# Four weight loads moved to another queue, and a later block's input made ahead of other steps

## The chip, the cores and the metric

The kernel runs on one core of a Trainium2 chip. Its engines are TensorE (PE in the profile, with its weight loads shown apart as PEld), VectorE (DVE), ScalarE (ACT), GpSimd (POOL) and SyncE (SP, which here only issues DMAs). The metric is the device time of one execution in microseconds (us); lower is better. Before the change the median of three runs is 349.3 us (348.23, 349.3, 350.38).

## The reference

A chunked linear attention (a decayed state scan) feeds a gated feed-forward layer.

```python
# x (4, 8, 768, 32), a (4, 8, 768), B and C (4, 8, 768, 16)
for c in range(768 // 32):
    cum = np.cumsum(la, axis=-1)                      # la = log of the clipped a
    L = np.exp(cum[..., :, None] - cum[..., None, :]) * causal
    M = np.einsum('bhin,bhjn->bhij', Cc, Bc) * L
    y_intra = np.einsum('bhij,bhjd->bhid', M, xc)
    y_inter = np.einsum('bhin,bhnd->bhid', Cc, state) * np.exp(cum)[..., None]
    y[:, :, sl] = y_intra + y_inter
    state = decay_full * state + sum_j(B_j x_j * decay_from_j)
# x = y as (3072, 256); w_gate, w_val (256, 1536); w_out (1536, 256)
g = x @ w_gate
out = (g * sigmoid(g) * (x @ w_val)) @ w_out
```

## The kernel before, in words

The 768 steps of the sequence are cut into six blocks of 128 (k = 0 to 5), each with all four batches, so a block's x for the feed-forward layer is 256 features by 512 tokens. The layer's 1536 hidden features are twelve groups of 128 (f = 0 to 11).

**Steps and their names.** Every piece of work is added to a planner (class `Plan`, lines 45 to 191) with a name, which is used below and in the lists of the code. For a block k of the attention: "L k b" is the decay scan of batch b on DVE, "S k" the scores on PE, "M k p" the mixing of scores and decays on DVE (`mix`, line 419), "y k" the values and carried part on PE (lines 519 to 549), "ap k q" a new state's copy out of PSUM, "step k q" the state recurrence on DVE (`step`, line 476, four instructions). The x that the layer reads is split into a high part "xh" and a low part "xl" (lines 574 and 586), each in four pieces i for k > 0. For the layer: "gv k f m" is the gate (m = 0) or value (m = 1) matmul group on PE (line 666), "si k f" the silu on ACT (line 677), "pr k f" the product on DVE (line 682); "hh" and "hl" are the high and low part of the hidden values, "po" the output matmuls. PSUM has four banks for gv and po, so gv 1 2 0 needs the bank that si 1 0 lets go.

**Weights.** There are 18 weight pieces of 512 KB: twelve for the gate and value weights (wg0 to wg11, i = 0 to 11) and six for the output weights (wo0 to wo5, i = 12 to 17). Each is 64-bit data from which the kernel makes a rounded high part and a low part. Its steps are "raw i" (the load, `w_fetch`, line 599), "mag i" and "rest i" (ACT, lines 606 and 620), "range i" (mostly POOL, line 616), "shift i", "sign i", "round i" (DVE, lines 627 to 637), "wh i" (ACT, line 639), for i < 9 "minus i" (ACT) and a POOL accumulating DMA "wl i", for the others "wl i" on DVE (line 647). The raw pieces share eight buffers (`RAW`), so a ninth load waits until the first piece's round has read its buffer; the working tile w of the output weights has one buffer, so mag 13 comes after wl 12. Block 0 uses the first nine groups in full fp32 from the piece's own tile, with x whole ("xf 0" to "xf 5", on ACT), and only from group 9 on the split form.

**Who sets the order.** SP issues the loads of raw 0 to 11 and the attention's inputs ("bc", "xb", "aj", and "E", the decays for the state, which has one buffer). Two DMAs that write the clipped decays back to DRAM, named "written" and "written e", and raw 12 to 17 are issued by ACT. The planner simulates all engines, takes the ready step of lowest rank at each point, and so writes one program order for each engine. `plan.follow(order)` makes each step of a list wait in the plan for the one before it to be issued; `plan.fix(e, names)` does so for an engine's own list. Lists for DVE, Act, Pool and PE stand in `FRONT` (lines 1000 to 1028) and hold until about 62 us of the run; after them, and on SP, ranks decide. Each engine then runs its instructions in that order. All engine calls go through the helper `Ordered`, whose line 202 is therefore the line of nearly every instruction in the profile.

Of the kernel before, what the change touches and what calls it, by code (L numbers as in the profile page):

```python
# [28 lines left out]
NF = DFF // P  # L29
# [15 lines left out]
class Plan:  # L45
# [19 lines left out]
    def add(self, engine, cost, run, rank, needs=(), takes=(), uses=(), gives=None, kind=None, lag=0.0, rows=1.0, slack=0.0):  # L65
        engines = [(engine, cost)] if cost is not None else engine
        self.ops.append(Op(engines, run, rank, needs, takes, uses, gives, kind, lag, rows, slack, cost is None))
# [145 lines left out]
def scan_moe_kernel(ctx: ExitStack, tc, aj, an, bc, xb, wgv, wo, cst, own, first_e, out):  # L213
    nc = tc.nc
    PSUM = bass.MemoryType.PSUM
    te, ve, se, ge, sp = (
        Ordered(tc, e) for e in (nc.tensor, nc.vector, nc.scalar, nc.gpsimd, nc.sync)
    )

    def pool(name, bufs, stack=ctx, **kw):  # L220
        return stack.enter_context(tc.tile_pool(name=name, bufs=bufs, **kw))
# [5 lines left out]
    raw = pool("raw", RAW)  # L227
# [323 lines left out]
    xh, xl = {}, {}  # L551
# [44 lines left out]
    NW = len(pieces)  # L596
# [50 lines left out]
    def w_low(i):  # L647
        _, his, los, j, name = pieces[i]
        hi = part[i]["hi"]
        if i < WHOLE:  # L650
            lo = part[i]["lo"]
# [14 lines left out]
    def gate_val(k, f, m):  # L666
        t = hid.setdefault((k, f), {})["gv"[m]] = ps_mm.tile([P, T], F32, tag="mm", name=f"gv{k}_{f}_{m}")
        if not k and f < WHOLE:
            w = part[f]["w"].bitcast(F32).rearrange("p (a b c) -> p a b c", b=2, c=P)
# [55 lines left out]
    rest = {}  # L725
# [29 lines left out]
    def do(f, *a):  # L755
        return lambda *e: f(*a, *e)


    plan = Plan(
        dict(mm=4, at=4, L=1, E=1, bc=1, xb=1, Cz=1, T=2, raw=RAW, w=1, xh=2, xl=2, sg=SG, ob=2),  # L760
        dict(SP=3.3, Act=3.0, DVE=1.0, PE=1.5, Pool=2.0, Page=0.0, **{"-": 0.7}),
    )
    add = plan.add
# [10 lines left out]
    def due(k, f=0):  # L774

        return begin[k] + f * (GV if k else PACE0)

    def at(n):

        return divmod(n, NF)  # L780

    def due_sum(k, f):
        return begin_sum[k] + f * PO
# [5 lines left out]
    for n, ranks in enumerate(IDLE):  # L789
        for i, r in enumerate(ranks):  # L790
            need = [("idle", n, i - 1)] if i else IDLE_AFTER[n]
            takes = [] if i else [("at", ("rest", n))]
# [2 lines left out]

    for i in range(NW):
        r = due(0, i) - 1.0 if i < NF else due_sum(0, 2 * (i - NF)) - 1.0
        if i < NF:
            add("SP", 0.48, do(w_fetch, i), r - 9.0, takes=[("raw", ("raw", i))], gives=("raw", i), lag=SHARED.get(i, 1.3))
        else:  # L800
            add("Act", 0.1, do(w_fetch, i, se), due(*at(LAST[i - NF])) + 2, [("si", *at(LAST[i - NF]))], takes=[("raw", ("raw", i))], gives=("raw", i), lag=1.3)
        add("Act", 0.57, do(w_magnitude, i, "Act"), r - 5.5, [("raw", i)], takes=[("sg" if i < NF else "w", ("w", i))], gives=("mag", i))
        far = i in FAR
        e, c = ("Pool", 2.2) if far else ("DVE", 0.335)
        add(e, c, do(w_range, i, ge if far else ve), r - 4.5, [("mag", i), *([("round", i - 1)] if i == 1 else [])], gives=("range", i))
        add("Act", 0.57, do(w_rest, i, "Act"), r - 4.5, [("raw", i), *([("xf", 5)] if i == 3 else [])], gives=("rest", i))
        add("DVE", 0.335, do(w_shift, i), r - 4.2, [("range", i)], gives=("shift", i))
        gate = ()
        if not i:
            n, gate = slice(0, 2 * P), [("round", 0, "gate")]  # L810
            add("DVE", 0.35, do(w_sign, i, n), r - 3.9, [("shift", i)], gives=("sign", 0, "gate"))
            add("DVE", 0.35, do(w_round, i, n), r - 3.3, [("sign", 0, "gate"), ("rest", i)], uses=[("raw", i)], gives=gate[0])
        n, c = (slice(2 * P, 4 * P), 0.35) if not i else (slice(0, 4 * P), 0.6)
        add("DVE", c, do(w_sign, i, n), r - 3.9, [("shift", i), *gate], gives=("sign", i))
        add("DVE", c, do(w_round, i, n), r - 3.3, [("sign", i), ("rest", i)], uses=[("raw", i)], gives=("round", i))
        if i < WHOLE:
            r = due(1, i) - LATER
        add("Act", 0.57, do(w_high, i, "Act"), r - 2.7, [("round", i), ("gv", 0, 0, 0)], gives=("wh", i))
        whole_done = [("gv", 0, i, m) for m in range(2)]
        if i < WHOLE:  # L820
            add("Act", 0.57, do(w_minus, i), r - 2.6, [("round", i), ("gv", *at(MINUS[i]), 0) if MINUS[i] else ("ap", 1, 1)], gives=("minus", i))
            add("Pool", 1.2, do(w_low, i), r - 2.5, [("wh", i), ("minus", i), *whole_done], uses=[("w", i)], gives=("wl", i), lag=1.6)
        else:
            add("DVE", 0.6, do(w_low, i), r - 1.5, [("wh", i)], uses=[("w", i)], gives=("wl", i))
# [10 lines left out]
    for k in range(NB):  # L835
        r = due(k)
        SLACK = min(k / 2, 1.0)
        z = -5 if not k else r + LEAD[min(k, 3)]
        L, E, BC, XB, CZ, TT = ("L", k), ("E", k), ("bc", k), ("xb", k), ("Cz", k), ("T", k)
# [14 lines left out]
        if not k:  # L854
# [4 lines left out]
            for b in range(BATCH):  # L859
                r = z + 0.5 + b  # L860
# [56 lines left out]
        if not k:  # L917
            add("-", 0.0, new_whole, -9, [("clip", 1)], takes=[("xl", "xf")], gives="xf")
            add("-", 0.0, do(new_x, 0), due(0, WHOLE) - 9, [("xf", i) for i in range(6)], takes=[("xh", ("xh", 0)), ("xl", ("xl", 0))], gives=("x", 0))
            for g in range(2):  # L920
                r = due(0, WHOLE) - 7 + 2 * g
                add("Act", 0.57, do(first_high, g, "Act"), r, [("x", 0)], gives=("xh", 0, g))
# [11 lines left out]
    for k in range(NB):  # L934
        xs = [(t, k, i) for t in ("xh", "xl") for i in range(2 * K if k else 2) if k or t == "xh" or not i]
        for f in range(NF):
            r = due(k, f)
# [14 lines left out]
            r = due_sum(k, f) - 4  # L952
# [4 lines left out]
        for n, (m, t, fs) in enumerate(sums_of(k)):  # L957
# [4 lines left out]
            r = due_sum(k, fs[0]) + n * 0.01  # L962
            c = 0.7 * len(fs) * (t[1] - t[0]) / T
            add("PE", c, do(project, k, m, t, fs), r, need, takes=[] if fs[0] else [("mm", b)], uses=[b, *(("h", k, f) for f in fs)], gives=prev, kind="r")
            if fs[-1] == NF - 1:
# [1 line left out]
                c = 0.6 * (t[1] - t[0]) / T  # L967
                add([("Act", c), ("DVE", c)], None, do(drain, k, m, t), r + 0.5, [prev], takes=[("ob", o)], uses=[b, o], gives=o)
                add("SP", 0.48, do(store, k, m, t), r + 2, [o], uses=[o], gives=("stored", k, m, t), lag=0.9)
    plan.follow([("raw", i) for i in range(NW)])  # L970
    for steps in ORDER:
        plan.follow(steps)
    for e, names in FRONT.items():
# [11 lines left out]
FETCH = dict(aj=10.0, an=35.0, bc=12.0, xb=31.0)  # L985
LATER = 3.0
WHOLE = 9
LAST = (5, 6, 9, 10, 11, 12)
MINUS = (3, 3, 4, 5, 5, 5, 10, 10, 10)
FEW = 8  # L990
# [13 lines left out]
sign 2, round 2, shift 3, sign 3, round 3, pr 0 1, shift 4, sign 4, round 4, step 0 1, shift 5, pr 0 2, sign 5, round 5,  # L1004
shift 6, sign 6, round 6, pr 0 3, shift 7, sign 7, round 7, shift 8, sign 8, pr 0 4, round 8, L 1 0, L 1 1, L 1 2, pr 0 5,
L 1 3, shift 9, bt 1, sign 9, M 1 0, pr 0 6, round 9, M 1 1, M 1 2, ce 1, M 1 3, pr 0 7, wl 9, shift 10, sign 10, round 10,
shift 11, pr 0 8, ap 1 0, wl 10, step 1 0, sign 11, round 11, pr 0 9, step 1 1, wl 11, shift 12, sign 12, round 12, pr 0 10,
xh 1 0, xh 1 2, xl 1 0, xl 1 1, xl 1 2, xl 1 3, wl 12, pr 0 11
""",
    Act="""  # L1010
by batch, Cz 0, mag 0, E 0, ap 0 0, rest 0, written, mag 1, xf 0, xf 1, xf 2, xf 3, xf 4, xf 5, rest 1, mag 2, rest 2, si 0 0,
mag 3, rest 3, mag 4, rest 4, mag 5, si 0 1, rest 5, mag 6, ap 0 1, written e, rest 6, mag 7, rest 7, si 0 2, mag 8, Cz 1, rest 8,
xh 0 0, si 0 3, xh 0 1, wh 0, minus 0, wh 1, minus 1, si 0 4, mag 9, rest 9, wh 2, minus 2, wh 3, si 0 5, raw 12, wh 4,
mag 10, rest 10, wh 5, wh 6, wh 7, wh 8, si 0 6, raw 13, minus x 0, minus x 1, mag 11, si 0 7, rest 11, minus 3, minus 4, wh 9,
si 0 8, mag 12, rest 12, rest 13, minus 5, wh 10, ap 1 1, si 0 9, raw 14, wh 11, si 0 10, raw 15, minus 6, minus 7, minus 8,
wh 12, xh 1 1, xh 1 3, rest 14, si 0 11, raw 16, mag 13, si 1 0, raw 17, hh 0 0, rest 15
""",
    Pool="""
clipped, range 0, range 3, range 4, range 5, range 6, range 7, range 8, wl 0, range 9, wl 1, wl 2, range 10, xl 0 0, range 11,
# [11 lines left out]
SHARED = {9: 6.1, "aj": 2.4, 10: 1.9}  # L1031
# [58 lines left out]
```

## Time and profile before

| | |
|---|---|
| median of three runs | 349.3 us (348.23 to 350.38) |
| profiled execution | 347.7 us, of which the span of the trace is 345.6 us |
| PE busy | 340.6 us (99%) |
| DVE busy | 225.9 us (65%) |
| ACT busy | 124.2 us (36%) |
| POOL busy | 45.5 us (13%) |
| chain that ended last | PE 86%, DVE 9%, issue 3%, DMA 1% |
| granted TensorE clock | full (1.0) over the span |

All times inside the profile are in us from the start of the span. A timeline row gives the start, the time taken, the engine, the operation, the tiles written and read (out<-in), and how many instructions were merged into the row. ACTq and SPq rows are the issues of DMAs, not the transfers. The instructions of one engine overlap a little: a 0.68 us DVE instruction is followed by the next one 0.60 us after its start.

### The profile page before, as it was taken

The numbers are of one execution on the slowest core, as the hardware profiler recorded it, in microseconds if no ns is written. First come the engines' busy times: TensorE is split into PE (matmuls) and PEld (weight loads), VectorE is DVE, ScalarE is ACT, GpSimd is POOL, SyncE is SP. The second block draws the span as 40 slices with busy tenths as digits, with TensorE's granted clock in tenths as the row PEclk, the third lists the DMA queues.
The fourth block names the chain that finished last, engine by engine and source line by source line (L and its number), as shares of the span: only waits on it lengthen the run. The fifth ranks groups of instructions, "written<-read, shape, count | busy, mean of one in ns | idle before, by whom it ended". The sixth has DMA issues, their size and how long they took to land.

```text
span 345.6 us, 7433 instructions
## 1 busy us (share of the span) xinstructions
PE 340.6 (99%) x3207; PEld 267.1 (77%) x3207; DVE 225.9 (65%) x399; ACT 124.2 (36%) x231; POOL 45.5 (13%) x36
## 2 busy tenths in 40 slices
PE   8999999999999999999999999999999999999996
PEld 7644457788788888887888878888888888888895
DVE  7999999979599763675582686454676440565320
ACT  4699766742445502212312212322222221222221
POOL 2389763220321000000000000000000000000000
PEclk9999999999999999999999999999999999999999
DMA  7899976980002811000651000392000000100001
GB/s 247 298 378 284 247 147 195 236 234 0 1 4 87 212 71 62 0 2 2 186 124 61 0 2 2 108 185 78 2 0 3 4 0 3 58 2 0 0 2 61
DMA packets 9983, 30.98 MB, mean 90 GB/s; under 512 B 1311, under 2 KB 2111, under 8 KB 9311
## 3 DMA queue, kind: packets, MB, share of 16 engines
q1 hardware_dynamic: 7192, 24.23, 23.2%
q0 software_dynamic: 1440, 2.88, 4.6%
q10 hardware_dynamic: 1319, 3.41, 3.1%
q8 instruction: 25, 0.41, 0.5%
q14 instruction: 7, 0.06, 0.1%
HBM read 24.28 MB, written 3.35 MB: 80 GB/s over the span
## 4 chain that ended last, share of the span: by engine, by line
PE 86%; DVE 9%; issue 3%; DMA 1%; ACT 0%; DVEq 0%; ACTq 0%
PE gv L202 49%; PE po L202 29%; PE y L202 4%; PE S L202 2%; DVE L L202 2%; DVE sg L202 2%; PE a L202 1%; DVE T L202 1%; DMA rows<-in_aj 1%; DVE wg4w L202 1%; DVE wg3w L202 0%; DVE wg5w L202 0%; DVE wg6w L202 0%; DVE wg9w L202 0%; DVE wg10w L202 0%
## 5 line engine op out<-in xcount | busy, mean ns | idle before, releaser
L202 DVE TENSOR_TENSOR sg<-gv,sg 128x512 f32<-128x512 f32 x72 | 49.6, 689 | 77.4 <-PE gv L202 76.6
L202 ACT ACTIVATE sg<-gv 128x512 f32<-128x512 f32 x72 | 43.1, 598 | 109.8 <-PE gv L202 109.8
L202 DVE TENSOR_TENSOR hh<-sg,hh 128x512 fp32r<-128x512 f32 x72 | 49.9, 696 | 13.5 <-ACT hh L202 12.3
L202 ACT CAST hh<-sg 128x512 fp32r<-128x512 f32 x31 | 19.3, 622 | 27.1 <-PE po L202 20.6
L202 DVE TENSOR_TENSOR_SCAN L<-L,dj 128x520 f32<-128x520 f32 x20 | 23.9, 1242 | 2.5 <-DMA L<-clipped 2.5
L202 ACT COPY ob<-po 128x512 f32<-128x512 f32 (+1 forms) x13 | 7.2, 555 | 48.6 <-PE po L202 48.1
L202 DVE CAST hh<-sg 128x512 fp32r<-128x512 f32 x41 | 17.4, 427 | 2.3 <-PE po L202 1.2
L202 DVE TENSOR_TENSOR L<-S,L 128x512 f32<-128x512 f32 x24 | 15.1, 682 | 0.3 <-PE S L202 0.3
L202 PE MATMUL po<-hh,wo4h 128*128 128x512 f32 (+1 forms) x52 | 15.2, 376 | 0.0
L202 PE MATMUL po<-hh,wo2h 128*128 128x512 f32 (+1 forms) x52 | 15.2, 375 | 0.0
L202 PE MATMUL po<-hh,wo0h 128*128 128x512 f32 (+1 forms) x52 | 15.2, 375 | 0.0
L202 PE MATMUL po<-hh,wo5h 128*128 128x512 f32 (+1 forms) x52 | 15.1, 373 | 0.0
L202 PE MATMUL po<-hh,wo3h 128*128 128x512 f32 (+1 forms) x52 | 15.0, 373 | 0.0
L202 PE MATMUL po<-hh,wo1h 128*128 128x512 f32 (+1 forms) x52 | 15.0, 373 | 0.0
L202 PE MATMUL y<-L,xb 64*32 64x64 f32 x768 | 11.3, 236 | 0.1
L202 PEld LDWEIGHTS y<-L,xb 64*32 64x32 f32 x768 | 9.2, 112 | 2.9 <-issue 2.1
L202 PEld LDWEIGHTS po<-hh,wo0h 128*128 128x128 f32 x52 | 9.5, 188 | 1.9 <-issue 0.2
L202 PEld LDWEIGHTS po<-hh,wo3h 128*128 128x128 f32 x52 | 9.5, 188 | 1.7
L202 PEld LDWEIGHTS po<-hh,wo5h 128*128 128x128 f32 x52 | 9.5, 188 | 1.7
L202 PEld LDWEIGHTS po<-hh,wo1h 128*128 128x128 f32 x52 | 9.5, 188 | 1.7
L202 PEld LDWEIGHTS po<-hh,wo2h 128*128 128x128 f32 x52 | 9.4, 188 | 1.8
L202 PEld LDWEIGHTS po<-hh,wo4h 128*128 128x128 f32 x52 | 9.4, 188 | 1.7
(302 smaller groups left out, 749.3 us busy)
## 6 DMA issues: line engine op xcount, KB each, us to landing
L<-clipped SPq DMA_DIRECT2D x10, 520.0 KB
xb<-in_xb SPq DMA_DIRECT2D x6, 768.0 KB, 11.1
bc<-in_bc SPq DMA_DIRECT2D x6, 512.0 KB, 3.3
out<-ob SPq DMA_DIRECT2D x11, 256.0 KB, 5.4
E<-clipped SPq DMA_DIRECT2D x5, 260.0 KB
wg0r<-in_wgv SPq DMA_DIRECT2D x1, 512.0 KB
wg1r<-in_wgv SPq DMA_DIRECT2D x1, 512.0 KB
wg2r<-in_wgv SPq DMA_DIRECT2D x1, 512.0 KB
```

Of the source, the lines that this page charges most:

```text
L202: ins = getattr(self.engine, name)(*a, **k)
```

## The change

The loads raw 4 to 7 go from SP's queue to ACT's, and leave SP's list; they stand in ACT's order at four places. In DVE's order the x of block 1 (the second block) comes ahead of step 1 1 and of shift, sign and round of piece 12; in ACT's order xh 1 1 and xh 1 3 come ahead of minus 8, and wh 12 behind raw 16.

```diff
     for i in range(NW):
         r = due(0, i) - 1.0 if i < NF else due_sum(0, 2 * (i - NF)) - 1.0
-        if i < NF:
+        if i in BESIDE:
+            add("Act", 0.1, do(w_fetch, i, se), r - 9.0, takes=[("raw", ("raw", i))], gives=("raw", i), lag=SHARED.get(i, 1.3))
+        elif i < NF:
             add("SP", 0.48, do(w_fetch, i), r - 9.0, takes=[("raw", ("raw", i))], gives=("raw", i), lag=SHARED.get(i, 1.3))
...
-    plan.follow([("raw", i) for i in range(NW)])
+    plan.follow([("raw", i) for i in range(NW) if i not in BESIDE])
+    plan.follow([("raw", i) for i in BESIDE])
...
+BESIDE = range(4, 8)
...
     DVE="""
...
-shift 11, pr 0 8, ap 1 0, wl 10, step 1 0, sign 11, round 11, pr 0 9, step 1 1, wl 11, shift 12, sign 12, round 12, pr 0 10,
-xh 1 0, xh 1 2, xl 1 0, xl 1 1, xl 1 2, xl 1 3, wl 12, pr 0 11
+shift 11, pr 0 8, ap 1 0, wl 10, step 1 0, sign 11, round 11, pr 0 9, wl 11, pr 0 10, xh 1 0, xh 1 2, xl 1 0, xl 1 2, xl 1 1, xl 1 3,
+step 1 1, shift 12, pr 0 11, sign 12, round 12, wl 12
 """,
     Act="""
-by batch, Cz 0, mag 0, E 0, ap 0 0, rest 0, written, mag 1, xf 0, xf 1, xf 2, xf 3, xf 4, xf 5, rest 1, mag 2, rest 2, si 0 0,
+by batch, Cz 0, mag 0, E 0, ap 0 0, rest 0, written, raw 4, mag 1, raw 5, xf 0, xf 1, xf 2, raw 6, xf 3, xf 4, xf 5, raw 7, rest 1, mag 2, rest 2, si 0 0,
...
-si 0 8, mag 12, rest 12, rest 13, minus 5, wh 10, ap 1 1, si 0 9, raw 14, wh 11, si 0 10, raw 15, minus 6, minus 7, minus 8,
-wh 12, xh 1 1, xh 1 3, rest 14, si 0 11, raw 16, mag 13, si 1 0, raw 17, hh 0 0, rest 15
+si 0 8, mag 12, rest 12, rest 13, minus 5, wh 10, ap 1 1, si 0 9, raw 14, wh 11, si 0 10, raw 15, minus 6, minus 7,
+xh 1 1, xh 1 3, minus 8, rest 14, si 0 11, raw 16, wh 12, mag 13, si 1 0, raw 17, hh 0 0, rest 15
```

## Rows read from the trace of the kernel before

**Rows 1.** Busy time by stretch: stretch, length, then each engine (x instructions).
```profile
36.65:48.29 11.64, 11.64 (x90) 5.45 (x89) 11.64 (x15) 9.09 (x18) 7.48 (x7) 1.00 0.96 220
48.29:60.90 12.61, 12.04 (x294) 9.54 (x293) 12.44 (x29) 7.05 (x16) 5.19 (x5) 1.00 0.65 167
```

**Rows 2.** Chain that ended last, in order of time: start, length, what.
```profile
60.90 33.04 PE gv L202 x144
```

**Rows 3.** Timeline at y 1: the last mix step, and PE's weight loads.
```profile
47.98 0.68 DVE L202 TENSOR_TENSOR L<-S,L 128x512 f32<-128x512 f32 x1
...
48.78 0.55 PEld L202 LDWEIGHTS y<-L,xb 64*32 64x32 f32 x45 [0.25 <-issue]
```

**Rows 4.** Timeline 55 to 62 us: the steps around block 1's x.
```profile
55.75 0.62 ACT L202 CAST wg11h<-wg11w 128x512 fp32r<-128x512 f32 x1 [2.35 <-DVE wg11w L202]
...
56.23 0.86 DVE L202 SCALAR_TENSOR_TENSOR T<-T,E 128x64 f32<-128x64 f32 x4
56.27 0.59 ACT L202 ACTIVATE sg<-gv 128x512 f32<-128x512 f32 x1
56.62 0.86 PE L202 MATMUL y<-L,xb 64*32 64x64 f32 x64
...
59.41 0.68 DVE L202 TENSOR_TENSOR sg<-gv,sg 128x512 f32<-128x512 f32 x1
...
59.83 0.61 PE L202 MATMUL gv<-xh,wg11l 128*128 128x512 f32 x2
60.01 0.74 DVE L202 CAST xh<-y 128x256 fp32r<-128x256 f32 x2
...
60.90 0.70 PE L202 MATMUL gv<-xh,wg0h 128*128 128x512 f32 x2 [0.45 <-DVE xh L202]
...
61.99 0.68 DVE L202 TENSOR_TENSOR wo0l<-wo0w,wo0h 128x512 fp32r<-128x512 f32 x1
```

**Rows 5.** Timeline: E's load, the next output piece and silu, weigh_c of block 2.
```profile
58.76 0.63 SPq L202 DMA_DIRECT2D E<-clipped  x1
...
62.77 0.67 ACT L202 ACTIVATE wo1w<-wo1r 128x512 f32<-128x512 f32 x1 [1.03 <-DVE wo0l L202]
...
63.35 0.58 ACT L202 ACTIVATE sg<-gv 128x512 f32<-128x512 f32 x1
...
84.66 0.69 DVE L202 TENSOR_TENSOR bc<-bc,E 128x512 f32<-128x512 f32 x1
```

**Rows 6.** Timeline of ACT at the start: "written", rest 0, the second xf group.
```profile
12.29 0.33 ACTq L202 DMA_DIRECT2D clipped<-all  x1
...
12.71 0.67 ACT L202 ACTIVATE wg0r<-wg0r 128x512 int32<-128x512 uint32 x1
...
14.85 0.76 ACT L202 COPY xf<-y 128x256 f32<-128x256 f32 x3 [0.33 <-PE y L202]
```

**Rows 7.** Transfers in 10 to 12.3, 12.3 to 16, 16 to 20, 20 to 24.
```profile
DMA packets 109, 0.37 MB, mean 159 GB/s; under 512 B 13, under 2 KB 21, under 8 KB 109
...
q1 hardware_dynamic: 317, 1.16, 97.7%
...
DMA packets 553, 1.63 MB, mean 407 GB/s; under 512 B 61, under 2 KB 181, under 8 KB 552
...
q10 hardware_dynamic: 135, 0.09, 7.5%
...
DMA packets 452, 1.67 MB, mean 417 GB/s; under 512 B 52, under 2 KB 52, under 8 KB 447
```

**Rows 8.** Timeline of SP's issues: raw 10.
```profile
22.34 0.33 SPq L202 DMA_DIRECT2D wg10r<-in_wgv  x1
```

**Rows 9.** Timeline 24 to 27 us: mag 7, si 0 2, pr 0 2.
```profile
23.95 0.67 ACT L202 ACTIVATE wg7w<-wg7r 128x512 f32<-128x512 f32 x1
...
25.07 0.60 ACT L202 ACTIVATE sg<-gv 128x512 f32<-128x512 f32 x1
...
26.99 0.68 DVE L202 TENSOR_TENSOR sg<-gv,sg 128x512 f32<-128x512 f32 x1
```

## The prediction

> **What bounds the kernel now.** I read the busy times by stage first. TensorE (PE) is busy in all 11.64 us between 36.65 and 48.29, and VectorE (DVE) too; between 48.29 and 60.90 PE is busy 12.04 of 12.61 us, DVE 12.44 [rows 1]. So PE sets the time, and DVE is close behind it until 60.9 us. Then I read the chain that ended last: back from the end it is PE alone as far as 60.90, where one piece of 33.04 us with 144 matmuls starts, 0.459 us for two [rows 2]. Ahead of 60.90 it runs through DVE. A gain must come from an idle moment of PE before that point, and a loss needs DVE, ScalarE (ACT) or a transfer to be late for PE.
>
> Two such moments are to be seen. At y 1, the values of the second block (k = 1), PE's weight loads pause 0.25 us before 48.78, just when DVE finishes the last mix step M 1 3 (47.98 + 0.68 = 48.66) [rows 3]. Here DVE has nothing to spare: what DVE loses earlier, PE loses here. The other is at 60.90: gv 1 0 0 waits 0.45 us for xh, which DVE made at 60.01; the second block's x was complete on PE at 56.62 + 0.86 = 57.48 already [rows 4]. This is the stall that the new DVE order can reach.
>
> **Second block's x made earlier.** The steps ahead of xh in DVE's list are now step 1 1, wl 11, shift 12, sign 12, round 12, pr 0 10. From 56.23 (step 1 1) to 59.41 (pr 0 10) is 3.18 us; one step of the 0.68 us form takes 0.60 from start to start (59.41 to 60.01), so without wl 11 the four moved steps hold 2.58 us [rows 4]. After the change only wl 11 and pr 0 10 stand there. wl 11 waits for wh 11, which ACT ends at 55.75 + 0.62 = 56.37: say 56.42. pr 0 10 follows at 57.02; its silu ends at 56.27 + 0.59 = 56.86. xh starts at 57.62, after y's end at 57.48; its two casts take 0.74, and casts and four xl together 1.98 (60.01 to 61.99, where wl 12 follows) [rows 4], so xh is complete at 58.36 and xl at about 59.6. ACT's two xh now precede minus 8 and can start near 57.9 as well. PE wants xh one pair after 59.83, at 60.29, and xl two pairs later, at 61.21. Both are ready 1.5 us or more before that. PE starts at 60.29 and not at 60.90: **0.61 us gained**, the most this part can give. Its lower bound is 0.
>
> **What the moved steps make late.** DVE starts step 1 1 at 59.60; with pr 0 11 now among them, the four moved steps take 2.58 + 0.60 to the next start, 62.78, and round 12 ends some 0.08 behind that, the overlap of the 0.68 us form: 62.86. step 1 1 is the last user of the single E buffer. E's load for the third block, issued by SP at 58.76, must wait for it until about 60.5, 1.7 us, and at worst xb's load behind it on SP as well. The first reader, ce 2 on DVE, is at 84.66 [rows 5]: 22 us of cover; at 0 in the sum. The state itself is read no earlier than the third block's carried part.
> Behind round 12 ACT is in order: wh 12 (0.62, as wh 11), then mag 13, which shares one buffer with wl 12 (0.68, DVE), then si 1 0. mag 13 started at 62.77, 0.10 after wl 12 ended (61.99 + 0.68 [rows 4]), and si 1 0 0.58 later, at 63.35 [rows 5]. That makes 62.86 + 0.05 + 0.62 + 0.05 + 0.68 + 0.10 + 0.58 = 64.94 for si 1 0, ended at 65.52 (0.58 long), against 63.93 now. It frees the bank that gv 1 2 0 needs, twelve pairs after 60.29, or 65.80. The cover is thus only 0.28 us, and each 0.1 us by which DVE or ACT run later than this costs PE 0.1. Bounds: 0 and 0.6; I take 0.1, since the sum of the spacings comes out just in time.
>
> **Four loads issued by ACT.** ACT gets four DMA issues of about 0.33 us: raw 4 and 5 around mag 1, raw 6 between xf 2 and xf 3, raw 7 after xf 5. If each held the engine up, the three before xf 3 would cost 1.0 us less the 0.33 that ACT idles there for PE [rows 6], and raw 7 another 0.33: up to 1.0 us. I take 0: the issue "written" of the same list stands behind rest 0, and yet it was issued at 12.29 while rest 0 began at 12.71 [rows 6]; ACT's sequencer is ahead of its engine, and each of the new issues has queued work in front of it. SP loses four issues, so raw 8 can go out right behind raw 3 while fresh buffers are left, and raw 7 then takes the buffer of raw 0, whose last reader is round 0; nothing that raw 7 waits for stands behind it on ACT. The start of gv 0 0 0 is set by xf, not by SP; nothing is gained there.
>
> **When the four pieces land.** raw 4 to 7 now come after raw 8. A piece is 0.524 MB. From 12.3 us the transfers moved 1.16, 1.63 and 1.67 MB up to 16, 20 and 24 us, after 0.37 MB between 10 and 12.3 [rows 7]. Served in order of issue (raw 2, 3, 8, written, 4, 5, 6, 7), raw 7 is complete with 7 x 0.524 + 0.09 = 3.76 MB, at 20 + 4 x (3.76 - 3.16) / 1.67 = 21.4. The old raw 7, sixth, is complete by the same count at 20.2; raw 10, for which the queue's waits name it as the last releaser, was issued at 22.34 [rows 8], so landing took 2.1 us more at most. So the new one lands by 23.5, and mag 7 is at 23.95 [rows 9]. By the same count raw 4 and 5 may keep ACT waiting some 1 us; si 0 2, the first of its steps that DVE would miss, has 1.3 us of cover (below). Cost 0.
> Order of issue is what the row says: "written", issued on ACT's queue at 12.29 [rows 6], moved nothing up to 16 us: all 317 packets of that window are of SP's q1, and the 135 of ACT's q10 came in the next [rows 7]. The Trainium skill, "DMA: Bandwidth & Descriptors", section "Queues, rings and completion order", says that each DMA engine takes turns between the queues it has work for, a packet each. This trace does not bear it out from the moment of issue; once q10's packets did flow, both queues moved at once, as it says. What turns would do here is the first rival.
>
> **Sum.** -0.61 + 0.1 + 0 = -0.5 us. The profiled execution took 347.7 us (span 345.6), 1.6 below the median of 349.3; a shift of the span applies to both: 347.2 there and 348.8 as the median. A measurement of this kernel can tell about 1%, 3.5 us, from no change.
>
> **Rivals.**
> *Late pieces, slower.* If ACT's queue and SP's shared one to one from raw 3 on, raw 7 would be complete when 0.524 + 2 x 2.19 = 4.9 MB have moved, just after 24 us (4.83 by then [rows 7]), and land with 2.1 more at 26.3: mag 7 2.35 us late. si 0 2 follows 1.12 behind and would end at 25.67 + 2.35 = 28.0; pr 0 2 stands in order on DVE at 26.99 [rows 9], 1.3 us of cover. DVE loses 1.05, has no slack up to M 1 3, and PE loses it at y 1: +1.05 - 0.5 = +0.5, 349.8. If the pieces also started as late as "written" did, after 16, and took 3 us each, mag 7 would come near 28.7, the loss would be 3.4 and the time 352.2. It decides from a landing at 25.3; slower than before from 25.9. For it: these are the pieces that were moved behind another. Against it: rows 7. Chance 0.12, with some 0.03 of it above 1%.
> *No gain, PE waits elsewhere.* The stall at 60.90 goes, but si 1 0 behind mag 13 is late by more than 0.28, and gv 1 2 0 gives the 0.6 back: 349.3. For it: the thin cover above; against it: the spacings, which come out in time by it. Chance 0.15.
> *Issues not hidden.* ACT holds xf up by some 0.7: -0.5 + 0.7 = +0.2, 349.5. Against it: rows 6. Chance 0.06.
> *More gained.* DVE, less hindered by GpSimd at other instants, also removes the 0.25 us at y 1 [rows 3]: -0.75 and, with a luckier order later, -1.2: 348.1. Chance 0.10.
> My forecast, a gain of 0.3 to 0.6: 0.57.
>
> **Numbers.** 348.8 us. Each case but the worst end of the first rival lies between 348.1 and 349.8; the three runs before spread 1.1 to either side of their median, so I take 346.9 to 350.6. Faster by over 1%: 0.02, since PE idles only 0.57 us in the stage [rows 1] and its work is untouched. Slower by over 1%: 0.04. Within: 0.94.
>
> **What would show it.** gv 1 0 0 directly behind gv 0 11 1, with no wait for xh, near 60.3; xh on DVE near 57.6; step 1 1 after xl, E's load near 60.5; ACT's four issues between 12.6 and 15.6 with xf and gv 0 0 0 still at 14.85 and 15.1; raw 8 on SP near 11.2; no wait of ACT for wg7r; PE's piece after 60.3 unbroken. Wrong would be: ACT waiting for wg6r or wg7r and DVE for si 0 2; a pause of PE at gv 1 2 0; or M 1 3 ending well after 48.7.

## The result and the profile after

The changed kernel took 354.03 us (median of 4 runs, 353.62 to 354.5) against 349.43 us for the kernel before on the same chip (4 runs, 348.23 to 350.38): a ratio of 1.0132, with an interval of 1.0098 to 1.0166. The forecast of 348.8 us and its range up to 350.6 were wrong; the change costs 4.6 us. Medians and ratios leave out single executions in a slower state of the chip; four of the kernels below have one such execution each. The profiled execution of after took 353.74 us with a span of 351.6 us, 6.0 more than the profiled span before; the pair differs by more than the medians because the profiled execution before, 347.7 us, is one of that kernel's faster ones.

The first view is the chain that ended last (start, length, what). Where it had been DVE and PE ahead of 60.90 [rows 2], it is now one transfer: raw 7, from its issue by ACT at 16.06 to ACT's first reading of it at 32.24.

```profile
16.06 16.16 DMA wg7r<-in_wgv
32.22 0.02 issue
32.24 0.66 ACT wg7w L202
32.90 0.55 ACT wg7r L202
33.45 0.49 ACT sg L202
...
33.98 9.90 PE gv L202 x16
...
64.32 35.59 PE gv L202 x156
```

The list of waits (who waited for whom: us in total, times, longest) shows three engines stopped by it, one behind the other. Before, ACT had no wait for any of the four pieces; after, it waits for raw 4 and raw 5 too (0.59 and 0.80 us).

```profile
DVE sg L202 <- ACT sg L202: 5.9, 1, 5.9
...
ACT wg7w L202 <- DMA wg7r<-in_wgv: 4.8, 1, 4.8
...
PE gv L202 <- ACT sg L202: 3.4, 1, 3.4
...
ACT wg6w L202 <- DMA wg6r<-in_wgv: 1.4, 1, 1.4
```

The timeline gives the places. The first three rows are mag 7, si 0 2 and pr 0 2, which answer to [rows 9]: 8.29, 8.28 and 6.97 us later than there. The fourth is gv 0 4, both groups. The last three are block 1's x on DVE, the last pair of gv 0 11 1 and the first of gv 1 0 0, which answer to [rows 4].

```profile
32.24 0.66 ACT L202 ACTIVATE wg7w<-wg7r 128x512 f32<-128x512 f32 x1 [4.83 <-DMA wg7r<-in_wgv]
...
33.35 0.58 ACT L202 ACTIVATE sg<-gv 128x512 f32<-128x512 f32 x1
...
33.96 0.69 DVE L202 TENSOR_TENSOR sg<-gv,sg 128x512 f32<-128x512 f32 x1 [5.87 <-ACT sg L202]
...
33.98 6.47 PE L202 MATMUL gv<-xf,wg4w 128*128 128x512 f32 x8 [3.40 <-ACT sg L202]
...
64.22 0.76 DVE L202 CAST xh<-y 128x256 fp32r<-128x256 f32 x2 [0.74 <-PE y L202]
...
66.65 0.62 PE L202 MATMUL gv<-xh,wg11l 128*128 128x512 f32 x2
...
67.10 0.62 PE L202 MATMUL gv<-xh,wg0h 128*128 128x512 f32 x2
```

PE lost time twice here. It waited 3.40 us for a bank that si 0 2 had to free, and then gv 0 4 took 6.47 us where the same eight matmuls take 3.60 elsewhere. The busy times by stretch (columns as in [rows 1]; the number after POOL is the granted clock) show why: after the pause, in which PE was busy 0.02 of 2 us, the clock was granted at 0.50, the lower level of 1.2 GHz, in all of 34 to 38 us and, by the means of 0.69 and 0.60, in parts of the stretches beside it.

```profile
32.00:34.00 2.00, 0.02 (x1) 0.02 (x1) 0.04 (x1) 1.76 (x4) 1.02 (x1) 0.69 0.99 252
34.00:38.00 4.00, 4.00 (x5) 1.84 (x6) 3.90 (x7) 4.00 (x8) 3.07 (x2) 0.50 0.73 281
38.00:40.00 2.00, 2.00 (x4) 0.82 (x3) 1.93 (x5) 2.00 (x5) 0.84 (x1) 0.60 0.28 97
```

How late PE is against before, at one piece after another, is the ledger of the change:

| PE starts | before | after | later by |
|---|---|---|---|
| gv 0 0 0 | 15.08 | 15.80 | 0.72 |
| gv 0 3 0 | 26.26 | 26.99 | 0.73 |
| gv 0 4 0 | 29.69 | 33.98 | 4.29 |
| gv 0 5 0 | 33.13 | 40.28 | 7.15 |
| y 1 1 | 55.78 | 62.61 | 6.83 |
| gv 1 0 0 | 60.90 | 67.10 | 6.20 |

So 3.56 are the wait (3.40 by the list), 2.86 the lower clock; 0.32 come back up to y 1 1, most of it at y 1, where M 1 3 is now done before PE gets there, and 0.63 at gv 1 0 0.

The transfers of 16 to 20, 20 to 24 and 24 to 28 us show how raw 7 came late (packets, MB, share of the 16 DMA engines' time; q1 is SP's queue, q10 ACT's).

```profile
q10 hardware_dynamic: 433, 1.21, 79.0%
q1 hardware_dynamic: 99, 0.34, 20.9%
...
q1 hardware_dynamic: 223, 0.85, 52.4%
q10 hardware_dynamic: 223, 0.81, 50.0%
...
q1 hardware_dynamic: 129, 0.73, 92.0%
q10 hardware_dynamic: 48, 0.15, 14.2%
```

Up to 20 us the older DMAs go first: SP's "bc" for block 1, issued at 15.97, hardly moves while ACT's raw 4 to 6, issued at 13.05 to 14.30, are served; most of q1's 99 packets there are raw 8's. From 20 to 24 both queues flow and take turns, 223 packets each. By 24 us q10 had moved 2.02 of the 2.19 MB it had been given ("written" and four pieces). Then SP's next transfer, L of block 1, gets in. In 24 to 28 the 129 packets of q1 took 92% of 64 engine-us, 0.46 us each, against 0.15 each in the stretch before; the trace has L's packets at 8,320 bytes and 0.5 to 0.9 us, the pieces' at 4,096 bytes and 0.16 us. The last 0.17 MB of ACT's pieces needed until 32 us.

### The profile page after: what moved, and what is told of

Its sections match the earlier page's. It is cut to its first block, busy times and chain, and to the rows that moved or that the text cites. A ratio compares the mean times of both kernels' runs of the same rounds, so it can differ in the third digit from the quotient of the medians.

```text
span 351.6 us, 7435 instructions
## 1 busy us (share of the span) xinstructions
PE 343.4 (98%) x3207; PEld 268.6 (76%) x3207; DVE 223.4 (64%) x396; ACT 126.3 (36%) x234; POOL 44.9 (13%) x36
## 4 chain that ended last, share of the span: by engine, by line
PE 89%; DMA 5%; ACT 1%; issue 0%; ACTq 0%
PE gv L202 55%; PE po L202 28%; DMA wg7r<-in_wgv 5%; PE y L202 4%; PE S L202 2%; ACT wg7w L202 0%; ACT wg7r L202 0%; ACT sg L202 0%; ACT ob L202 0%; ACTq L202 0%
## 5 line engine op out<-in xcount | busy, mean ns | idle before, releaser
L202 DVE TENSOR_TENSOR hh<-sg,hh 128x512 fp32r<-128x512 f32 x72 | 49.7, 696 | 13.9 <-ACT hh L202 12.7
L202 ACT CAST hh<-sg 128x512 fp32r<-128x512 f32 x33 | 20.5, 622 | 22.3 <-PE po L202 14.7
```

What stands on the lines that cost most here:

```text
L202: ins = getattr(self.engine, name)(*a, **k)
```

## The experiments

**The two halves apart.** First the order half alone: all loads on SP as before.

```diff
-BESIDE = range(4, 8)
+BESIDE = range(0)
-... written, raw 4, mag 1, raw 5, xf 0, xf 1, xf 2, raw 6, xf 3, xf 4, xf 5, raw 7, rest 1, ...
+... written, mag 1, xf 0, xf 1, xf 2, xf 3, xf 4, xf 5, rest 1, ...
```

> Only the second half of the change: the new order of DVE and ACT around the second block's x; raw 4 to 7 are issued by SP as before. If the four moved loads are the whole loss, PE has no wait at gv 0 4 0, gv 1 0 0 follows gv 0 11 1 without a pause, and the time is 0.4 to 0.7 us below the kernel before (near 348.9, ratio 0.998). If the new order has a part in the loss, it is slower than before by 0.5 us or more.

Measured: 349.47 us, ratio 1.0009 (0.998 to 1.0038). The expected gain, 0.2% of the time, is smaller than this interval can show. The profiled span is 345.2, 0.4 less than before, and gv 1 0 0 follows gv 0 11 1 with no wait. But in ACT's part of the timeline a new wait stands, of which more below:

```profile
59.95 0.62 PE L202 MATMUL gv<-xh,wg11l 128*128 128x512 f32 x2
...
60.40 0.61 PE L202 MATMUL gv<-xh,wg0h 128*128 128x512 f32 x2
...
72.97 0.66 ACT L202 ACTIVATE wo4r<-wo4r 128x512 int32<-128x512 uint32 x1 [4.39 <-DMA wo4r<-in_wo]
```

The loads half alone has the lists of before from step 1 1 and minus 8 on:

```diff
-... round 11, pr 0 9, wl 11, pr 0 10, xh 1 0, xh 1 2, xl 1 0, xl 1 2, xl 1 1, xl 1 3, step 1 1, shift 12, pr 0 11, ...
+... round 11, pr 0 9, step 1 1, wl 11, shift 12, sign 12, round 12, pr 0 10, xh 1 0, xh 1 2, xl 1 0, ...
-... minus 7, xh 1 1, xh 1 3, minus 8, rest 14, si 0 11, raw 16, wh 12, mag 13, ...
+... minus 7, minus 8, wh 12, xh 1 1, xh 1 3, rest 14, si 0 11, raw 16, mag 13, ...
```

> Only the first half: raw 4 to 7 issued by ACT, the old order of DVE and ACT around the second block's x. If the loads are the whole loss: ACT waits 4 to 5 us for wg7r, PE 3 to 4 us for si 0 2, and the time is the changed kernel's plus the 0.6 us that the new order saves, near 354.6, 5.2 above before. If the two halves share the loss: 3 us above before or less.

Measured: 353.14 us, 1.0119 (1.0078 to 1.016), span 351.0; the 354.6 expected was 1.5 too high. ACT waits 4.42 us for raw 7, mag 7 starts at 32.03, and a wait for xh, 0.55 us, is back. As far as these intervals tell, the whole loss is the loads'.

**L out of the way.** All of the change stays; only SP's order is altered, so that L of block 1 goes out behind raw 11.

```diff
-    [("raw", 8), ("bc", 1), ("raw", 9), ("aj", 1), ("raw", 10), ("xb", 1), ("raw", 11), ("E", 1)],
+    [("raw", 8), ("bc", 1), ("raw", 9), ("raw", 10), ("xb", 1), ("raw", 11), ("aj", 1), ("E", 1)],
```

> The changed kernel with one edit of SP's order: the two loads of L for the second block are issued behind raw 11 and not behind raw 9. Theory: raw 7 is late because the packets of ACT's queue take turns with those of SP's, and its last ones alternate with L's packets of 8,320 bytes, 0.6 us and more each. Then raw 7 lands by 26 us and not at 32.2, ACT waits under 1.5 us for it, PE's wait at gv 0 4 0 is under 0.7 us, and the time is within 1.5 us of the kernel before (348.5 to 351), unless L is now late for its scans near 37 us. Rival: raw 7 is late because it was issued late (16.06 us, behind xf 5) and stands behind raw 8; then it lands near 32 as before and the time stays near 354.

Measured: 350.42 us, 1.0042 (1.0016 to 1.0068), span 348.1. From this run's timeline and waits:

```profile
27.70 0.68 ACT L202 ACTIVATE wg7w<-wg7r 128x512 f32<-128x512 f32 x1 [0.74 <-DMA wg7r<-in_wgv]
...
30.05 3.60 PE L202 MATMUL gv<-xf,wg4w 128*128 128x512 f32 x8
```
```profile
DVE L L202 <- DMA L<-clipped: 4.3, 3, 1.7
...
PE gv L202 <- DVE sg L202: 1.7, 2, 1.1
```

mag 7 comes at 27.70 instead of 32.24 (the theory had raw 7 landed by 26), and PE no longer waits at gv 0 4, nor is its clock lowered. Now L is late in its turn for DVE's scans; PE's waits for DVE, 1.7 us and 0.77 at y 1, make most of the 2.9 us by which the span is above that of the order half alone. Without L, mag 7 is 4.5 us earlier than in after; of its 3.75 us against before (27.70 against 23.95) L is not the cause, and SP's smaller transfers flow beside it in that time.

**Was the lowered clock a cost of its own?** Fifteen idle 128x512 matmuls ahead of gv 0 4 keep PE busy through the wait; they use no data of the result.

```diff
-gv 0 3 1, gv 0 4 0,
+gv 0 3 1, idle 2 0, idle 2 1, ... idle 2 14, gv 0 4 0,
```

> The changed kernel with 15 matmuls of 128x512 bf16 without use in PE's order ahead of gv 0 4 0, 3.4 us of work for the time in which PE waits there. If the eight matmuls of gv 0 4 take 6.47 us and not 3.60 because the granted clock fell after the wait, they take 3.6 to 3.8 here while ACT's wait for wg7r stays near 4.8 us, and the time falls by 2 to 3 us, to 351 to 352. If they are slow for another reason (transfers, waits for single weights), they stay near 6.5 and the time near 354.

Measured: 353.89 us, 1.0142 (1.01 to 1.0185): no gain. PE's and DVE's timeline:

```profile
33.40 0.69 DVE L202 TENSOR_TENSOR sg<-gv,sg 128x512 f32<-128x512 f32 x1 [6.32 <-ACT sg L202]
33.41 3.70 PE L202 MATMUL gv<-xf,wg4w 128*128 128x512 f32 x8 [0.32 <-ACT sg L202]
...
53.84 0.64 PE L202 MATMUL y<-L,xb 64*32 64x64 f32 x42 [0.77 <-DVE L L202]
```

The clock stayed at full and gv 0 4 took 3.70 us, but a wait came back at y 1, where DVE, whose pr 0 2 was 6.4 us late (33.40 against 26.99), had not mixed the scores. gv 1 0 0 started at 65.36, 1.74 us earlier than in after, but 0.60 of that is raw 7's landing (mag 7 at 31.64). So of the 2.86 us of lower clock only some 1.1 counted; the rest lay beside DVE's own lateness. Of the 1.74 us 1.07 were lost again by the scores of block 2 (99.24 against 99.91), 0.77 of them at gv 1 5 0, behind the same wait for raw 16 as above. The loads half says the same without idle matmuls: PE was late there before (its gv 0 0 took 6.10 us, last section), so it waited only 0.77 us at gv 0 4 and kept its clock, but then waited 0.77 at y 1 for DVE, and the span is 351.0 all the same. DVE's lateness and PE's are two bounds of nearly one height; my expectation saw only one.

**Is it the number of pieces, or ACT's queue?** Three loads on ACT's queue, raw 7 back on SP:

```diff
-BESIDE = range(4, 8)
+BESIDE = range(4, 7)
-xf 5, raw 7, rest 1
+xf 5, rest 1
```

> The changed kernel with raw 7 back on SP, right behind raw 3; raw 4 to 6 stay on ACT's queue. Theory: raw 7 is early now, so no wait for it; raw 4 to 6 still take turns with SP's pieces and ACT waits 2 to 3 us for the three together, of which si 0 2's 1.3 us of cover take a part; DVE loses 1 to 2 us at pr 0 2 and the span is 346 to 347.5. If only L's large packets matter, the waits are under 1 us in all and the span is 345.5 or less. If any load on ACT's queue costs the same, the span is near 350.

Measured: 353.27 us, 1.0123 (1.0084 to 1.0163), from three executions. The span is 350.5, 3 us above the theory's range and near the third case's 350. But the loads on ACT's queue did not cost the same: ACT waited 0.78 us for raw 4, 1.29 for raw 5 and 3.41 for raw 6. Now raw 6 is the last on ACT's queue. It was issued at 15.19, since it became the ninth load and had to wait for a buffer, and ACT's waits read:

```profile
ACT wg6w L202 <- DMA wg6r<-in_wgv: 3.4, 1, 3.4
...
PE gv L202 <- ACT sg L202: 1.5, 2, 0.9
```

Next, all on SP's queue, but raw 8 ahead of the four as in the change:

```diff
-BESIDE = range(4, 8)
+BESIDE = range(0)
-    plan.follow([("raw", i) for i in range(NW) if i not in BESIDE])
+    plan.follow([("raw", i) for i in (0, 1, 2, 3, 8, 4, 5, 6, 7, *range(9, NW))])
-    [("raw", 8), ("bc", 1), ("raw", 9), ...
+    [("raw", 7), ("bc", 1), ("raw", 9), ...
```

> The changed kernel with raw 4 to 7 issued by SP, in the order that the pieces have in the change: raw 2, 3, 8, 4, 5, 6, 7, then bc 1 and raw 9. raw 7 is behind raw 8 and waits for raw 0's buffer as in the change, and is issued near 15; only the second queue is gone. Theory (turns between two queues): raw 7 then lands where the seventh piece landed before, by 24, ACT waits under 0.5 us for pieces 4 to 7 together, and the span is that of the new order alone, near 345.3. Rival (place in the order and late issue): ACT waits 3 us or more for wg7r, span 349 or more.

Measured: 349.6 us, 1.0008 (0.998 to 1.0036). raw 7 was issued at 15.19 and mag 7 ran at 25.30 without a wait: the later place in one queue costs nothing that can be measured, and neither does the later issue. The span of 346.4 is above the 345.3 expected, with 0.8 us of it in gv 0 0 (4.51 for 3.70, last section). And last, the four loads on ACT as in the change, but raw 7 issued ahead of raw 8:

```diff
-... written, raw 4, mag 1, raw 5, xf 0, xf 1, xf 2, raw 6, xf 3, xf 4, xf 5, raw 7, rest 1, ...
+... written, raw 4, raw 5, mag 1, raw 6, xf 0, xf 1, xf 2, raw 7, xf 3, xf 4, xf 5, rest 1, ...
     plan.follow([("raw", i) for i in BESIDE])
+    plan.follow([("raw", 7), ("raw", 8)])
```

> The changed kernel with all four loads still on ACT's queue, but issued earlier (raw 4, raw 5, mag 1, raw 6, three xf, raw 7) and raw 8 of SP made to follow raw 7, as in the old order. If what is issued first on either queue is also started first, raw 7 now stands ahead of raw 8, bc 1 and raw 9, lands by 22.5, ACT waits under 1 us in all and the span is 345 to 346, so ACT's queue as such is harmless. If turns are taken with whatever SP issues later, raw 7 lands at 25 or later and the span is 348 or more. xf may be held up by up to 0.5 us by the issues in front of it.

Measured: 349.15 us, 1.0009 (0.9984 to 1.0034), and no wait of ACT for any of the four pieces. The span of 346.7 is above the 346 expected; 1.0 us of it is gv 0 0, which took 4.71 here:

```profile
14.58 0.41 ACTq L202 DMA_DIRECT2D wg7r<-in_wgv  x1
15.24 0.33 SPq L202 DMA_DIRECT2D wg8r<-in_wgv  x1
...
25.60 0.66 ACT L202 ACTIVATE wg7w<-wg7r 128x512 f32<-128x512 f32 x1
```

Its transfers show ACT's queue in 20 to 24 us and SP's in 24 to 28, where ACT's has none:

```profile
q10 hardware_dynamic: 83, 0.27, 16.8%
...
q1 hardware_dynamic: 137, 0.90, 105.6%
```

In after, ACT's queue still moved 48 packets in 24 to 28, beside L. ACT's queue as such costs nothing either. What costs most is a last piece on one queue that is still unfinished when the other queue reaches L: 1.48 us in the time of issue (14.58 against 16.06), with raw 8 moved out of the way, made 6.6 us at mag 7 (25.60 against 32.24).

**Where the order half's gain may go.** The pause at y 1 [rows 3] was the other idle moment of PE. M 1 3 is put ahead of ce 1 (the weighing of the block's C by its decays on DVE) on top of the order half alone:

```diff
-M 1 1, M 1 2, ce 1, M 1 3, pr 0 7
+M 1 1, M 1 2, M 1 3, ce 1, pr 0 7
```

> The new order of DVE and ACT alone (loads on SP) with one more edit in DVE's order: M 1 3 ahead of ce 1, which y 1's first half does not read. If PE's pause of 0.25 us inside y 1 is a wait for M 1 3, it goes, and the span is 0.1 to 0.25 us below the order alone: near 345.0, 0.6 below the span of before. If the pause has another reason it stays. In the median this is at the edge of what can be told.

Measured: 349.5 us, 0.9994 (0.9967 to 1.002). The pause at y 1 is gone, yet this profiled execution has a span of 348.8:

```profile
75.07 0.65 ACT L202 ACTIVATE wo4r<-wo4r 128x512 int32<-128x512 uint32 x1 [6.42 <-DMA wo4r<-in_wo]
...
76.26 0.83 PE L202 MATMUL gv<-xh,wg5h 128*128 128x512 f32 x2 [2.01 <-ACT sg L202]
```

rest 16 waits for raw 16, si 1 3 stands behind it on ACT, and gv 1 5 0 needs the bank that si 1 3 frees. Behind PE's pause the granted clock fell here, too: its mean is 0.80 over 72 to 80 us. The order half's own execution, with 4.39 us of ACT's wait, shows no such pause of PE. Before, rest 16 stood two silus further back and ran at 74.07 without a wait. Behind the lists of the change the planner placed it ahead of si 1 3. My first theory was again L: in the order half SP issues L of block 2 at 58.2, just ahead of raw 16 at 59.3. Two kernels put L behind E, one on the order half alone, one on the kernel with M 1 3 earlier:

```diff
 ORDER = (
+    [("E", 2), ("aj", 2)],
```

> The order half alone, with one thing more: the third block's scan decays (L of k = 2, two transfers) are issued behind E of k = 2 instead of ahead of it. In the order half alone raw 16, issued by ACT at 59.29 us, flows beside these L transfers (58.16 on SP's queue), ACT waits 4.39 us for it at rest 16 (72.97), and si 1 3 stands behind. Theory (a piece on ACT's queue is held by L's large packets of SP's queue here too): E waits for step 1 1 until 60.6, so L goes out near 61.3, raw 16 lands about 2 us earlier and ACT's wait for it falls from 4.4 to about 2 us or less; the span stays at 345.2 or a little under, and the median comes to 348.4 to 349.0, at or just below the kernel before. Rival (raw 16's landing does not depend on L): ACT's wait stays between 4 and 5 us.

> The same edit on the kernel that also has M 1 3 ahead of ce 1. There the profiled execution lost 2.0 us of PE at gv 1 5 0, behind si 1 3, behind rest 16, for which ACT waited 6.42 us (raw 16 issued 59.40, L 58.20). Theory: ACT's wait falls to 4 us or less, the wait of PE for a silu goes, and the span is 344.7 to 345.2 against 348.8; median 348.2 to 349.0. Rival (the 2.0 us are chance of that execution and raw 16's landing does not depend on L): ACT waits 4 us or more as before, and the median stays at 349.5.

Measured: 348.88 us, 0.999 (0.9965 to 1.0015), and 348.8 us, 0.998 (0.9949 to 1.0011). ACT's waits for raw 16 were 6.2 and 4.8 us, not 2 and 4, so that theory fell: ACT reads the piece 15.5 and 14.1 us after its issue with L behind it, 13.7 and 15.7 with L ahead. PE still paused at gv 1 5 0, by 1.84 and 0.44 us. But neither kernel takes L away: it was issued at 61.48 and 62.43, some 2 us behind raw 16, and transfers issued behind a piece were just what held raw 7. What sets raw 16's time stays open. The other remedy leaves the transfers alone and puts rest 16 back:

```diff
 ORDER = (
+    [("si", 1, 4), ("rest", 16)],
```

> The kernel with M 1 3 ahead of ce 1, with the transfers as they are and only ACT's order mended: rest 16 behind si 1 3 and si 1 4, where the kernel before has it. Theory (raw 16 lands at 73 to 75 and only what stands behind rest 16 in ACT's order makes it cost): no PE wait for a silu near 76, ACT's wait for raw 16 1 us or less, span 344.7 to 345.2, median 348.2 to 349.0. Rival (PE's loss near 76 has another cause): the median stays at 349.5 and PE still waits there.

Measured: 347.54 us, ratio 0.9967 (0.9944 to 0.999), the only kernel here that is measurably faster than the one before. Its profiled span, 347.2, is above the 345.2 expected by what its gv 0 0 took longer. Its timeline and its chain:

```profile
15.61 5.84 PE L202 MATMUL gv<-xf,wg0w 128*128 128x512 f32 x8
...
76.78 0.66 ACT L202 ACTIVATE wo4r<-wo4r 128x512 int32<-128x512 uint32 x1
```
```profile
60.02 35.59 PE gv L202 x156
```

rest 16 has no wait, and PE runs from 60.02 in one piece. Last, the same line on the order half alone, without the move of M 1 3:

> The order half alone (all loads on SP, M 1 3 where it was), with rest 16 behind si 1 3 and si 1 4 on ACT. Executions of the kernel before fall into two groups, near 348.0 and near 350.3 us, and those of the kernel with M 1 3 earlier and rest 16 later near 347.0 and 349.4. Theory (the order half gains 0.5 to 0.6 us at block 1's x, and in the order half alone this was hidden by rest 16 waiting for raw 16 ahead of si 1 3; the earlier M 1 3 adds 0.25 to 0.4): groups near 347.4 and 349.7, median 347.4 to 348.8, no PE wait for a silu near 76, the pause of 0.25 at y 1 still there. Rival (the whole gain is that of the earlier M 1 3): groups where the kernel before has them, 348.0 and 350.3.

Measured: 349.41 us against 350.2 for the kernel before in the same runs, 0.9983 (0.996 to 1.0005). The size fits the 0.6 us, but the interval just includes no change, and the median lies above the 348.8 expected, as that of the kernel before does above its earlier ones. Its profiled span is 345.1, with the piece behind y 1 1 unbroken (35.58 us) and the pause at y 1 still there.

## Why the prediction was wrong

**The step that failed** is "When the four pieces land". It counted the bytes ahead of raw 7 in order of issue, ended the list with raw 7 itself (complete at 21.4, landed by 23.5) and set the cost at 0. The order of issue holds for when a DMA starts: up to 20 us the trace of after shows it again. It doesn't hold once two queues flow. Then SP's transfers issued behind raw 7 come in beside it, and these were not in the count at all: "bc" and raw 9, and above all L with its long packets, which SP, relieved of four loads, issued at 18.51. In the runs raw 7 was ready for ACT at 32.24, and the cost of 0 was 4.6 us. In the first 24 us the trace of before had "written", 0.09 MB, as the only sample, and I read from 135 small packets what four pieces of 0.524 MB would do. Later on the same trace held the answer. ACT's loads raw 12 and raw 17 (wo0 and wo5, first two lines: size, time from issue to landing) took 6.3 and 13.9 us, and from 68 to 72 us, where ACT's output pieces flowed, ACT's, SP's and GpSimd's queue (q0) had 121, 122 and 121 packets:

```profile
wo0r<-in_wo ACTq DMA_DIRECT2D x1, 512.0 KB, 6.3
...
wo5r<-in_wo ACTq DMA_DIRECT2D x1, 512.0 KB, 13.9
...
q10 hardware_dynamic: 121, 0.43, 38.7%
q1 hardware_dynamic: 122, 0.45, 36.7%
q0 software_dynamic: 121, 0.23, 30.8%
```

By the Trainium skill, "DMA: Bandwidth & Descriptors", section "Queues, rings and completion order", each DMA engine takes turns between queues packet by packet. I set that aside, because the trace did not bear it out from the moment of issue. The 223 and 223 packets of 20 to 24 us now do bear it out for the time after both flow.

**The rival "Late pieces, slower"** was the right mechanism with the wrong size and a chance of 0.12. Its worst end put mag 7 at 28.7; it came at 32.24, since the rival, too, counted equal packets and stopped before L. Its price rule held: a loss of the landing less 25.3 gives 6.9 us, and pr 0 2 was 6.97 us late. "DVE has no slack up to M 1 3" was too strict: M 1 3 came 5.59 us late (53.57 against 47.98), so DVE made up 1.4. That PE would also wait by itself, and be slowed by the clock after it, stood in no case. The range is a little tighter than its own numbers: 349.8 and a spread of 1.1 make 350.9, not 350.6; that changes nothing here.

**Block 1's x** was right to a tenth: 0.61 forecast, 0.63 in the ledger. What the moved steps make late was right in kind, with the wrong instruction: I watched si 1 0 behind mag 13, where no run shows a pause, and the planner's free part moved rest 16 ahead of si 1 3 instead. I had followed only what the lists name. "No gain, PE waits elsewhere" came true in this form in the kernels with M 1 3 earlier or L behind E, where PE paused. In the order half alone ACT waited, but its profiled execution has no pause of PE, so that its gain went this way is not shown; the interval alone could hide it.

**ACT's issues at no cost** was right: with the four issues on ACT, gv 0 0 0 started at 15.80 in after but at 15.08, as before, in the kernel with the idle matmuls; with all loads on SP it started anywhere from 15.22 to 15.63. The rows account for the 0.72 of the ledger without ACT: 0.41 stand on PE at the step "e" already (9.77 against 9.36), ahead of the first of the four issues at 13.05, and 0.31 come from y 0's last two parts, which took 1.21 and 0.65 us against 1.09 and 0.46, at the lower clock (last section).

## What to carry to other kernels

Moving loads to a second queue makes them share with whatever the first queue issues next, so count what is issued behind the moved piece as well, with the time of its packets, until the piece has landed. A last small rest can take longest: 0.17 MB took 8 us beside L. A trace with one queue at work in the place of interest may have two at work in another: read the turns there. And where a planner fills in the order behind a hand-written list, compare the whole order of each engine, above all a step that waits for a DMA and has moved ahead of one that PE needs.

## What the runs showed of the hardware that was not expected

The first gate group, gv 0 0, takes unequal time: 3.70 us in eight of the fourteen profiled executions (before and after among them), 4.51 to 4.71 in four, 5.84 in that of the fastest kernel and 6.10 in the loads half's, with the granted clock column at 1.00 in each that was read. The weight loads tell why. The first two rows are of the fastest kernel's gv 0 0, the third of gv 0 4 in after, where the clock column says 0.50, and the last two of y 0 in the kernel before:

```profile
17.48 0.34 PEld L202 LDWEIGHTS gv<-xf,wg0w 128*128 128x128 f32 x1 [0.52 <-issue]
...
20.44 0.19 PEld L202 LDWEIGHTS gv<-xf,wg0w 128*128 128x128 f32 x1 [0.24 <-issue]
...
35.85 0.34 PEld L202 LDWEIGHTS gv<-xf,wg4w 128*128 128x128 f32 x1 [0.52 <-issue]
...
13.03 0.52 PEld L202 LDWEIGHTS y<-bc,T 32*64 32x64 f32 x16 [0.17 <-ACT T L202]
...
14.69 0.32 PEld L202 LDWEIGHTS y<-bc,T 32*64 32x64 f32 x16
```

A load that takes 0.19 us at the full clock takes 0.34 at the lower level, with the same gap of 0.52 ahead of it in both kernels. So TensorE ran at 1.2 GHz up to about 20 us in the fastest kernel's execution, and up to between 13 and 14.7 us in that of before: the column's 1.00 does not hold for the start of the span. PE was busy without a break from 8 us on in both; why the clock rose some 5 us apart was not tried. This is large enough to part the executions of one kernel: the fastest kernel's profiled execution, with 5.84, took 349.37 us, while six of its twelve took 346.87 to 347.18; the 2.14 us more in gv 0 0 would be most of that difference, though none of the six has a trace to show it. Where PE waits for raw 7 anyway, it is absorbed: in the loads half gv 0 0 took 2.40 us longer than in after, and gv 0 4 started at 33.77 against 33.98.

That a rest of 0.17 MB took from 24 to 32 us is more than turns of one packet each explain: from 25 to 30 us the trace has only one to four of ACT's 4,096-byte packets in each microsecond, beside 15 to 28 of L's. By the Trainium skill, "DMA: Bandwidth & Descriptors", section "Queues, rings and completion order", an engine drains a whole packet of some 9 to 17 descriptors before it changes queue. If what the profile counts are descriptors, a turn of L would take, at 0.65 us each, an estimated 6 to 11 us by that page's figure. No run here shows how they are bundled, nor on how many of the 16 engines the rest lay.
